# One quarter of a batch's denominators inverted on GpSimd by a power instead of on VectorE by a reciprocal

## The chip, the cores and the metric

The kernel runs on one core of one Trainium2 chip. Its time is device microseconds of one execution. Besides timed runs there is one profiled execution, from which all the durations and starts below come; starts count from the first instruction of that execution.

## The reference

The inputs are q, k and v, each of shape 4 x 6080 x 256 (batch, positions, channels), a number tau = 1, and two weight matrices. For each of the four batches the columns of q and k are normalized over the positions, a 256 x 256 matrix of channel products is formed, a softmax is taken over its rows, and v is multiplied by the result. All rows then go through a two-layer network with a tanh-approximated GELU.

```python
qn = q / (np.linalg.norm(q, axis=1, keepdims=True) + 1e-06)
kn = k / (np.linalg.norm(k, axis=1, keepdims=True) + 1e-06)
s = kn.transpose(0, 2, 1) @ qn / tau
s = s - s.max(-1, keepdims=True)
a = np.exp(s)
a /= a.sum(-1, keepdims=True) + 1e-09
x = (v @ a).reshape(B * S, D)                 # 24320 x 256
h = x @ w_in                                  # 24320 x 2048
g = 0.5 * h * (1.0 + np.tanh(c * (h + 0.044715 * h * h * h)))
out = g @ w_out                               # 24320 x 256
```

## The kernel before

**Stages.** The softmax matrix of a batch is small, so the kernel multiplies its exponentials into w_in once per batch (tiles `aw`, lines 454 to 474, scaled by the reciprocal row sums) and then applies the result to v directly. The main loop runs over 48 blocks of 512 positions (12 per batch, the last of each 448 wide). For a block n, TensorE computes the hidden layer from `aw` and the transposed v block (`h`, line 521; some parts by a scheme with fewer products, `rb` and `qp`, line 597), ScalarE applies the GELU, and TensorE multiplies by w_out (`r` and `p`, line 726). VectorE forms the sums and differences that these schemes need, and turns the output blocks round.

**The next batch is prepared meanwhile.** While the blocks of one batch are worked on, the channel products of the next are accumulated from its q and k (line 248, `row` steps). Around the last two blocks of a batch stands a chain of small steps for the next one: the sums of squares (`ss`, `sv`), their square roots as a power 0.5 on GpSimd (`pow`, line 382, 128 x 4 elements), factors (`kf`, `kr`, `krp`), scaled products (`S0`, `S1`) and then the exponentials.

**The exponentials of later batches.** ScalarE has the table of the GELU loaded, which also gives tanh. For batches 1, 2 and 3 the exponential of a score x is therefore formed as (1 + t) / (1 - t) with t = tanh(x / 2), in `scores_c`:

- step `dn` (line 424, ScalarE): the denominators 1 - t, one tile of 128 x 512 float32.
- steps `rc0` to `rc3` (line 434, VectorE): each inverts a quarter of that tile in place, 128 x 128 elements.
- step `eT` (line 429, VectorE): (1 + t) times the inverted denominators, written as bfloat16.

Behind them come `rsum` (line 444, TensorE: the row sums of eT), `rs` (line 450, VectorE: their reciprocals), and the `aw` products (line 461, TensorE), all of which read eT or what comes of it. Batch 0 uses the exponential itself and has none of these steps.

**What sets the order.** The order is written out by hand: for each of the 48 blocks a string lists the steps, and every step issues its instructions at once, so each engine's queue holds them in the order of that list. An engine works through its queue in order and waits at an instruction until what it needs is there. In the three blocks concerned the relevant part of the list is

```
g0 w0cq rc0 w0y5 ... M1A-1 rc1 y5-1 ... M6A-1 rc2 G3 ... w1m5 rc3 w1m1 ... w1y5 eT w1m6 ... rsum+1 ...
```

(batch 1; `dn` is the third step before the end of the block before. In batches 2 and 3 `dn` and `rc0` to `rc3` stand in the same block as `eT`.)

**GpSimd's queue** holds, apart from the three square roots, the issues of DMAs: q and k tiles of the next batch (line 99, `lq` and `lk`) and the copies of v blocks into bfloat16 (line 153, `lv`, four blocks ahead). SyncE's queue holds the transposing loads of v (line 163) and the output stores (line 816).

Of the kernel before, what the change touches and what calls it, by code (L numbers as in the profile page):

```python
# [11 lines left out]
FP32 = mybir.dt.float32  # L12
BF16 = mybir.dt.bfloat16
AF = mybir.ActivationFunctionType
ALU = mybir.AluOpType
# [3 lines left out]
def kernel(  # L19
# [10 lines left out]
    nc = tc.nc  # L30
# [17 lines left out]
    const = ctx.enter_context(tc.tile_pool(name="const", bufs=1))  # L48
# [369 lines left out]
    def scores_c(b, step):  # L418

        th = TH[b]  # L420
        if step == 0:
            dn = smx.tile([128, 2, 256], FP32, tag="S", name=f"dn{b}")
            DN[b] = dn
            nc.scalar.activation(dn, th, AF.Copy, scale=-1.0, bias=1.0)
            return
        dn = DN[b]
        if step == 5:
            eT = smx.tile([128, 2, 256], BF16, tag="eT")
            nc.vector.scalar_tensor_tensor(eT, th, 1.0, dn, op0=ALU.add, op1=ALU.mult)
            ET[b] = eT  # L430
            return
        step -= 1
        piece = dn[:, step // 2, step % 2 * 128 : step % 2 * 128 + 128]
        nc.vector.reciprocal(piece, piece)

    DN = {}

# [383 lines left out]
    with tc.manual_schedule():  # L821
# [12 lines left out]
        nc.vector.memset(eps, 1e-12)  # L834
        halves = const.tile([128, 4], FP32)
        nc.vector.memset(halves, 0.5)
        log_it = const.tile([128, 1], FP32)
        nc.vector.memset(log_it, math.log(inv_tau))
        ident_bf = const.tile([128, 128], BF16)
# [45 lines left out]
        for f0, f1 in ((0, 256), (256, 512), (512, 1024), (1024, 1536), (1536, 2048)):  # L885
# [14 lines left out]
            "gc": g_copy, "ss": ss_cols, "sv": norms, "pow": roots, "kf": k_factors, "kr": k_row,  # L900
            "krp": k_row_pe, "rsum": row_sums, "rs": row_factors,
            "dn": lambda b: scores_c(b, 0), "eT": lambda b: scores_c(b, 5),
        }
        for i in range(2):
# [4 lines left out]
        for i in range(4):  # L909
            CHAIN[f"rc{i}"] = lambda b, i=i: scores_c(b, i + 1)  # L910
# [327 lines left out]
```

## Time and profile before

| | |
|---|---|
| timed runs | 696.82 and 696.54 us, median 696.68 |
| span of the profiled execution, first to last instruction | 695.2 us (the profile gives no other time for this execution) |
| instructions | 14413 |
| mean granted TensorE clock | 0.998 |
| TensorE busy | 677.3 us, 5501 matmuls |
| VectorE busy | 630.8 us, 1245 instructions |
| ScalarE busy | 616.0 us, 894 instructions |
| GpSimd busy | 73.4 us, 135 instructions |

The two timed runs lie 1.5 us above the span at their median; what lies outside the span is before the first and after the last instruction. In the lines of the profile PE is TensorE, PEld its weight loads, DVE VectorE, ACT ScalarE, POOL GpSimd and SP SyncE; `L434` is line 434 of the kernel; `out<-in` are the names of its tiles. A number in square brackets in a timeline is how long the engine was idle before the instruction and, behind the arrow, what ended that idleness. A line of "..." marks lines left out.

### The profile page before, as it was taken

How to read it: one execution, taken by the hardware profiler on the slowest of the kernel's cores; microseconds unless marked ns; L12 is line 12 of the kernel's file. 1: busy time of each engine (PE TensorE's matmuls, PEld its weight loads, DVE VectorE, ACT ScalarE, POOL GpSimd, SP SyncE). 2: the span in 40 equal slices, each digit the busy share in tenths (PEclk: the TensorE clock that was granted, in tenths of full speed). 3: DMA queues.
4: the chain of work that ended last, by engine and by line, in shares of the span. 5: the costliest groups of instructions: out<-in, count | busy, mean ns of one | idle time of the engine just before them, and what ended most of it. 6: DMA issues, size and time to landing. Idle time of an engine off the chain costs nothing.

```text
span 695.2 us, 14413 instructions
## 1 busy us (share of the span) xinstructions
PE 677.3 (97%) x5501; PEld 530.7 (76%) x5501; DVE 630.8 (91%) x1245; ACT 616.0 (89%) x894; POOL 73.4 (11%) x135
## 2 busy tenths in 40 slices
PE   3999999999999999999999999999999999999996
PEld 2857787777778777777777777777877888888785
DVE  3579998999998889999999889999999999999996
ACT  5389989999889999999988999999888999999993
POOL 4321101111001001101010100010000000000000
PEclk9999999999999999999999999999999999999999
DMA  9996888897478777747587777593563463453325
GB/s 240 207 269 98 160 141 126 114 150 109 65 144 126 130 120 105 122 80 121 91 138 121 119 120 126 97 141 53 83 99 69 77 103 61 81 103 59 54 39 89
DMA packets 161462, 79.07 MB, mean 114 GB/s; under 512 B 148448, under 2 KB 152160, under 8 KB 160672
## 3 DMA queue, kind: packets, MB, share of 16 engines
q0 software_dynamic: 14448, 39.72, 34.2%
q1 hardware_dynamic: 145696, 37.14, 31.8%
q10 hardware_dynamic: 1248, 1.28, 0.6%
q8 instruction: 43, 0.70, 0.4%
q14 instruction: 27, 0.22, 0.1%
HBM read 78.91 MB, written 36.57 MB: 166 GB/s over the span
## 4 chain that ended last, share of the span: by engine, by line
PE 95%; DMA 4%; DVE 0%; issue 0%; POOL 0%; ACT 0%; DVEq 0%; POOLq 0%
PE r L726 24%; PE h L521 22%; PE p L726 18%; PE rb L597 13%; PE qp L597 10%; PE G L248 5%; DMA t<-in_k_dram 2%; PE awp L461 2%; DMA t<-in_q_dram 1%; PE ss L282 0%; PE ss L275 0%; PE vt_ps L325 0%; PE rk L406 0%; PE warm L370 0%; DVE vT_pe L331 0%
## 5 line engine op out<-in xcount | busy, mean ns | idle before, releaser
L726 PEld LDWEIGHTS <-wcomb 128*128 128x128 bf16 x2688 | 261.9, 98 | 43.5 <-issue 0.2
L531 ACT ACTIVATE g<-h 128x1024 bf16<-128x1024 f32 (+1 forms) x178 | 179.9, 1014 | 16.4 <-PE h L521 13.9
L726 PE MATMUL r<-t,wcomb 128*128 128x256 bf16 (+1 forms) x1152 | 163.6, 272 | 0.1
L521 PE MATMUL h<-vT,aw 128*128 128x512 bf16 (+1 forms) x624 | 158.6, 377 | 0.0
L623 ACT ACTIVATE g<-qp 128x1024 bf16<-128x1024 f32 (+1 forms) x103 | 104.7, 1016 | 7.3 <-PE qp L597 5.8
L726 PE MATMUL p<-g,wcomb 128*128 128x256 bf16 (+1 forms) x760 | 108.0, 272 | 0.0
L521 PEld LDWEIGHTS <-aw 128*128 128x128 bf16 x712 | 69.2, 98 | 49.4 <-DVE aw L364 0.6
L597 PEld LDWEIGHTS <-sw 128*128 128x128 bf16 x824 | 80.2, 98 | 25.5 <-issue 1.3
L193 ACT ACTIVATE sq<-t 128x1536 bf16<-128x1536 bf16 (+4 forms) x59 | 79.2, 1359 | 6.2 <-DMA t<-in_q_dram 6.0
L618 DVE TENSOR_TENSOR qp<-rb,yw 128x512 f32<-128x512 f32 (+1 forms) x103 | 70.8, 688 | 12.3 <-PE rb L597 9.5
L597 PE MATMUL rb<-tv,sw 128*128 128x256 bf16 (+1 forms) x412 | 78.0, 271 | 0.2 <-DVE qp L618 0.2
L621 DVE TENSOR_TENSOR xw<-rb,yw 128x512 f32<-128x512 f32 (+1 forms) x103 | 69.5, 674 | 3.9 <-PE rb L597 2.4
L613 ACT ACTIVATE qp<-rb 128x512 f32<-128x512 f32 (+1 forms) x103 | 59.7, 580 | 11.9 <-PE rb L597 6.8
L597 PEld LDWEIGHTS <-aw 128*128 128x128 bf16 x618 | 60.3, 98 | 12.7 <-issue 0.7
L631 ACT ACTIVATE g<-xw 128x512 bf16<-128x512 f32 (+1 forms) x103 | 63.4, 626 | 1.3 <-DVE xw L621 1.2
L616 ACT ACTIVATE yw<-qp 128x512 f32<-128x512 f32 (+1 forms) x103 | 61.2, 594 | 3.7 <-PE qp L597 1.9
L699 DVE TENSOR_TENSOR t<-g,t 128x1024 bf16<-128x1024 bf16 (+1 forms) x96 | 63.4, 668 | 0.6
L701 DVE TENSOR_TENSOR t<-g 128x1024 bf16<-128x1024 bf16 (+1 forms) x96 | 63.8, 673 | 0.0
L703 DVE TENSOR_TENSOR t<-t,g 128x1024 bf16<-128x1024 bf16 (+1 forms) x96 | 63.6, 669 | 0.0
L628 ACT ACTIVATE g<-rb 128x512 bf16<-128x512 f32 (+1 forms) x103 | 61.2, 596 | 2.2 <-PE rb L597 1.7
L248 PE MATMUL G<-t 128*128 128x256 bf16 (+1 forms) x352 | 60.1, 279 | 0.1
L687 DVE TENSOR_TENSOR t<-g 128x2048 bf16<-128x2048 bf16 (+1 forms) x48 | 57.5, 1197 | 0.0
(137 smaller groups left out, 890.0 us busy)
## 6 DMA issues: line engine op xcount, KB each, us to landing
out_dram<-ot SPq DMA_DIRECT2D x174, 128.0 KB, 3.2
vb<-in_v_dram POOLq DMA_DIRECT2D x41, 256.0 KB, 4.2
t<-in_q_dram POOLq DMA_DIRECT2D x21, 384.0 KB, 4.9
t<-in_k_dram POOLq DMA_DIRECT2D x21, 384.0 KB, 5.8
wst<-in_moe_w_out_dram POOLq DMA_DIRECT2D x2, 1024.0 KB, 11.0
t<-in_q_dram POOLq DMA_DIRECT2D x3, 512.0 KB, 14.4
t<-in_k_dram POOLq DMA_DIRECT2D x3, 512.0 KB, 17.2
out_dram<-ot SPq DMA_DIRECT2D x12, 112.0 KB, 2.6
```

The lines of the kernel that those rows point to most:

```text
L193: nc.scalar.activation(o, t[:np_, r, :], AF.Square)
L248: nc.tensor.matmul(G[b][:, jc, :], lhsT=qt[:np_, r, jc * 128 : jc * 128 + 128], rhs=kt[:np_, r, :], start=first and jc == 0, stop=jc == 1, ...
L521: mm = nc.tensor.matmul(hp[:, u, :cols], lhsT=AW[b][:, cc, fc * 128 : fc * 128 + 128], rhs=vt_tiles[n][:, cc, :cols], start=cc == 0, stop= ...
L531: nc.scalar.activation(gs(n)[:, 2 * p : 2 * p + 2, :cols], HP.pop((n, p))[:, :, :cols], AF.Gelu_apprx_tanh)
L597: GATE[0] = nc.tensor.matmul(acc[:, u * hc : u * hc + hc], lhsT=lhs[:, u * 128 : u * 128 + 128], rhs=rhs, start=m in (1, 5) and u == 0, st ...
L618: nc.vector.tensor_add(qp(n, i)[:, 1, :c], RB[n, i][:, :c], YW[n, i][:, :c])
L621: nc.vector.tensor_add(XW[n, i][:, :c], RB[n, i][:, :c], YW.pop((n, i))[:, :c])
L623: nc.scalar.activation(gs(n)[:, 2 * pa : 2 * pa + 2, :c].rearrange("p u (t x) -> p t u x", t=2), QP.pop((n, i))[:, :, :c].rearrange("p t ( ...
L631: nc.scalar.activation(gs(n)[:, 2 * pb : 2 * pb + 2, hc:c], two(XW.pop((n, i))[:, :c]), AF.Gelu_apprx_tanh)
L701: nc.vector.tensor_sub(o, quarter(n, 1, 1, f0, f1), quarter(n, 0, 1, f0, f1))
L703: nc.vector.tensor_sub(o, ts[2][:, f0:f1, :hc], quarter(n, 1, 0, f0, f1))
L726: nc.tensor.matmul(ACCS[n, acc][:, :hc], lhsT=wcomb[:, w, fc, :], rhs=x, start=first and k == 0, stop=k == 3, skip_group_check=True)
```

## The change

In each of batches 1, 2 and 3 the first quarter of the denominators (step `rc0`) is inverted by GpSimd, as a power with exponent -1, and no longer by VectorE's reciprocal. The exponents are a constant tile of 128 x 128 elements, filled with -1 once at the start by VectorE. The other three quarters and all other steps stay; `rc0` stays at its place in the hand-written order. On GpSimd's queue the power thus stands in front of the DMA issues that follow it in that order, and `eT` now needs a result of GpSimd besides those of VectorE and ScalarE.

```diff
@@ scores_c
         step -= 1
         piece = dn[:, step // 2, step % 2 * 128 : step % 2 * 128 + 128]
-        nc.vector.reciprocal(piece, piece)
+        if step == 0:
+            nc.gpsimd.tensor_tensor(piece, piece, minus, op=ALU.pow)
+        else:
+            nc.vector.reciprocal(piece, piece)
@@ constants
         nc.vector.memset(halves, 0.5)
+        minus = const.tile([128, 128], FP32)
+        nc.vector.memset(minus, -1.0)
```

## Prediction

> **What bounds the kernel now.** I read the page's busy shares and chain first: they say which engine sets the end.
>
> ```profile
> PE 677.3 (97%) x5501; PEld 530.7 (76%) x5501; DVE 630.8 (91%) x1245; ACT 616.0 (89%) x894; POOL 73.4 (11%) x135
> ...
> PE 95%; DMA 4%; DVE 0%; issue 0%; POOL 0%; ACT 0%; DVEq 0%; POOLq 0%
> ```
>
> TensorE is busy for 677.3 of 695.2 us and is 95% of the chain that ended last. VectorE works 91% but almost never ends a wait on that chain, and GpSimd is nearly free. So VectorE time taken away is worth little, while a stop that reaches TensorE is paid in full: its queue is in order, and it has only 17.9 us of idle time in the whole span.
>
> Next, the tile view of the denominators (dn), and then that of rt, which the only power on GpSimd writes: after the name come the count and the shortest, median and longest duration in ns.
>
> ```profile
> L434 DVE RECIPROCAL dn<-dn x12: 894/942/954, 176.2 to 514.8; 128x128 f32<-128x128 f32 x12
> L424 ACT ACTIVATE dn<-th x3: 627/630/631, 175.5 to 508.8; 128x512 f32<-128x512 f32 x3
> L429 DVE SCALAR_TENSOR_TENSOR eT<-th,dn x3: 644/669/692, 182.8 to 516.9; 128x512 bf16<-128x512 f32 x3
> ```
>
> ```profile
> L382 POOL TENSOR_TENSOR rt<-sv,halves x3: 1028/1037/1049, 167.3 to 494.4; 128x4 f32<-128x4 f32 x3
> ```
>
> The reader is to see two durations side by side: a reciprocal of 128 columns takes VectorE 0.94 us; a power of four columns takes GpSimd 1.037 us.
>
> Last, the timeline around the first of the three batches (start and duration in us).
>
> ```profile
> 176.18 0.95 DVE L434 RECIPROCAL dn<-dn 128x128 f32<-128x128 f32 x1
> 177.29 0.70 DVE L618 TENSOR_TENSOR qp<-rb,yw 128x512 f32<-128x512 f32 x1 [0.16 <-ACT yw L616]
> ...
> 180.43 0.53 POOL L99 DMA_DIRECT2D t<-in_q_dram  x1 [10.23 <-ACT g L623]
> ...
> 182.57 0.51 POOL L153 DMA_DIRECT2D vb<-in_v_dram  x1 [1.62 <-PE rb L597]
> 182.80 0.64 DVE L429 SCALAR_TENSOR_TENSOR eT<-th,dn 128x512 bf16<-128x512 f32 x1
> ...
> 183.66 0.24 PE L444 MATMUL sums<-ones_bf,eT 128*128 128x1 bf16 x4
> ```
>
> The first piece is inverted at 176.18, as soon as ScalarE's dn is done (175.52 + 0.63 = 176.15), and its consumer eT starts at 182.80. TensorE reads eT for the row sums at 183.66, having waited 0.2 us for it (the tile view's figure). Behind that read the chain has no slack.
>
> **Part by part.**
>
> *Removed:* three reciprocals of 0.94 us on VectorE, 2.8 us in all. In the first batch VectorE then waits 0.16 us for ScalarE's yw anyway, and TensorE is the chain, so of these 2.8 us I count a gain of 0; the ends are 0 and -2.8.
>
> *Added, a constant:* one fill of 128x128 with -1 at the start. The fills of that size beside it take 0.17 us, and VectorE then idles 4.0 us for ident. Nothing; uncovered it would be 0.17.
>
> *Added, three powers of 128x128 on GpSimd.* No row shows one, so its duration d is bounded. From below: all of the 1.037 us is a fixed price, and more columns cost what they cost a plain GpSimd fill: 0.10 us at one column, 0.273 at 128, so 0.0014 us each; d = 1.04 + 124 x 0.0014 = 1.2 us. From above: everything is per column, d = 1.037 x 32 = 33.2 us. The rows nearest to the fixed price are the one-column fill (0.10) and ident's select of 128 columns (0.29 in all). With 0.10 fixed, a column costs 0.234 us and d = 30.0; with 0.29, 0.187 and d = 24.2. I take the middle, **d = 27 us**, because rows of simple work show that starting an instruction on GpSimd costs 0.1 to 0.3 us; the other 0.75 or more must be arithmetic of four columns, unless the power has a long preamble of its own. No row excludes one.
>
> *The new wait.* Square root's power started 0.09 us after its input (sv ended at 167.19), so the first batch's power starts at 176.25. The eT instruction now waits for it, and it stands in VectorE's in-order queue; TensorE's next instruction that needs eT, the row sums, stands in TensorE's. Both engines stop, and with them ScalarE and all that waits for products. Cover is the time from the power's start to eT's old start, less 0.1 for the signal: 182.80 - 176.25 - 0.1 = 6.45 us in the first batch; in the others (dn done at 343.64 and 509.45, eT at 351.20 and 516.87) 7.36 and 7.22. With d = 27 the delays are 20.55, 19.64 and 19.78: 60.0 us. In the second and third batch TensorE came to the sums 0.1 and 0.2 us after eT; less 0.3 gives 59.7.
>
> *TensorE after a stop.* The timeline's start shows what idleness does to it.
>
> ```profile
> 16.88 3.73 PE L248 MATMUL G<-t 128*128 128x256 bf16 x16
> ...
> 22.08 1.91 PE L248 MATMUL G<-t 128*128 128x256 bf16 x16
> ```
>
> The same sixteen matmuls take 3.73 us and later 1.91. Up to 14.98 us it worked in short bursts; working without pause from then on, it kept the slow rate until about 20.2: 5.2 us at half rate lose 2.6. After a stop of 20 us I add that three times: 7.8 (ends 0 and 7.8).
>
> *Queued behind the power on GpSimd* are DMA issues: t from q (180.43 before) and vb (182.57). They leave after 203.3, against 180.43 + 20.55 = 201.0 had they moved with everything else: 2.3 us late. The next squaring of a q tile is at 216.88, and vb is transposed a window (some 14 us) later. Nothing; without that cover, up to 2.3 us a batch. SyncE's queue holds nothing that moves.
>
> *Sharing between VectorE and GpSimd.* [...]
>
> ```profile
> 167.28 1.05 POOL L382 TENSOR_TENSOR rt<-sv,halves 128x4 f32<-128x4 f32 x1 [4.62 <-DVE sv L376]
> ...
> 167.84 0.68 DVE L701 TENSOR_TENSOR t<-g 128x1024 bf16<-128x1024 bf16 x1
> ```
>
> L701 reads two tiles and starts in the middle of the power. It takes 0.68 us, against 0.673 in the mean, and the power 1.05 against 1.03 and 1.04 in the batches where nothing of that kind overlapped it. So I count 0 for contention. [...]
>
> [...]
>
> **Sum.** 0 + 0 + 59.7 + 7.8 + 0 = 67.5 us on the profiled span of 695.2: 762.7. The median of the two timed runs, 696.68, is 1.5 above that span, so **764 us**, slower by 9.7%. With d = 24.2 it is 756, with 30.0 773, with 33.2 783; without the slow restart 756.
>
> **Rivals.**
>
> *A: the power costs mostly a fixed price (not slower).* For: the row has only one size, and a preamble of 0.8 us would explain it; GpSimd is idle 89%. Against: no other GpSimd row shows so dear a start. It decides at d = 6.45 us, or 0.044 us a column: below that the wait is covered, and the time is 696.7 with at most 2.8 gained: 694 to 697, likeliest 696.4, as TensorE's wait of 0.2 us is what could go.
>
> *B: in between, 0.05 to 0.16 us a column.* A loop that overlaps columns would give, say, d = 11: delays 4.55 + 3.64 + 3.78 = 12.0, and with stops this short perhaps no slow restart: 709. At d = 20, 39 + 7.8: 743. It covers 700 to 750.
>
> [...]
>
> *D: TensorE's clock does not fall* is inside the forecast's range: 756.
>
> **Chances.** Forecast 0.55 (d of 24 to 33 without exclusion: 748 to 783, counting restarts of 0 to 2.6 us), A 0.20, B 0.12, C 0.13. Within 2%, about what a measurement of this kernel can tell from no change (682.7 to 710.6), lies A and the lower end of B: 0.22. Slower 0.77. Faster would need 14 us from a VectorE that gives up 2.8: 0.01. The range: 695 to 787. It takes in A, since its 0.20 is too much to leave out beside the upper tails, and all of B and C but C's dearest end; the likeliest case alone is 748 to 783.
>
> **What would show it.** In the profile after: a row of three GpSimd powers of 128x128 near 27 us each; a wait of VectorE's eT on it of some 20 us, three times, and of TensorE's L444 behind it; slices of the span with lower busy digits at 176, and later twice more; half-rate matmuls after each. [...] If the power takes under 6.4 us, the forecast is wrong at its first step.

## The result and the profile after

The changed kernel takes 744.21 us (743.47 and 744.94) against 696.68: a ratio of 1.068, interval 1.065 to 1.071. Timed again in four executions it took 744.58 us, ratio 1.069 (1.067 to 1.070). The profiled execution has a span of 741.6 us where the kernel before had 695.2: 46.4 us more.

The page of the kernel after, its busy shares, the 40 slices of the span for TensorE, VectorE, GpSimd and TensorE's granted clock, and the chain that ended last:

```profile
PE 683.4 (92%) x5501; PEld 533.6 (72%) x5501; DVE 629.0 (85%) x1243; ACT 616.3 (83%) x894; POOL 135.7 (18%) x138
...
PE   3999999998399999999849999999966999999996
...
DVE  4589998997398899999739898999946999999997
...
POOL 4411011106601001101651001010083000000000
PEclk9999999999699999999969999999997999999999
...
PE 86%; POOL 8%; DVE 2%; DMA 1%; ACT 1%; issue 0%; SPq 0%; DVEq 0%; POOLq 0%; ACTq 0%
```

There are three holes in TensorE and VectorE; at each of them GpSimd is busy, and in the slice in which each hole ends TensorE's granted clock (the share of its full clock that it was allowed, `PEclk`) is down to 6 or 7 tenths. GpSimd, which was on none of the chain, has 8% of it: 62.4 us, the three powers. TensorE has the same 5501 matmuls.

The tile view of dn, the instructions that write it and eT (count, and shortest, median and longest in ns):

```profile
L437 DVE RECIPROCAL dn<-dn x9: 912/942/945, 177.6 to 545.8; 128x128 f32<-128x128 f32 x9
...
L435 POOL TENSOR_TENSOR dn<-dn,minus x3: 20802/20802/20803, 175.9 to 540.6; 128x128 f32<-128x128 f32 x3
L429 DVE SCALAR_TENSOR_TENSOR eT<-th,dn x3: 691/691/691, 196.8 to 561.4; 128x512 bf16<-128x512 f32 x3
```

And who waited for whom, in us in total, number of times, and the longest:

```profile
PEld L447 <- DVE eT L429: 41.4, 3, 14.3
DVE eT L429 <- POOL dn L435: 41.1, 3, 14.2
PE sums L447 <- DVE eT L429: 40.3, 3, 14.0
```

A power of 128 x 128 takes 20.80 us, 22 times the reciprocal that it replaces. eT waits 41.1 us for the three of them, and the row sums wait 40.3 us for eT. (Lines behind the edit have moved by three: the row sums are L447 here, L444 before.)

The timeline around the first batch, as before the change:

```profile
175.95 20.80 POOL L435 TENSOR_TENSOR dn<-dn,minus 128x128 f32<-128x128 f32 x1 [6.01 <-ACT dn L424]
...
178.48 0.63 DVE L702 TENSOR_TENSOR t<-g,t 128x1024 bf16<-128x1024 bf16 x1
...
180.48 0.63 DVE L704 TENSOR_TENSOR t<-g 128x1024 bf16<-128x1024 bf16 x1
...
196.73 0.60 POOL L99 DMA_DIRECT2D t<-in_q_dram  x1
196.78 0.69 DVE L429 SCALAR_TENSOR_TENSOR eT<-th,dn 128x512 bf16<-128x512 f32 x1 [14.19 <-POOL dn L435]
...
197.53 0.27 PE L447 MATMUL sums<-ones_bf,eT 128*128 128x1 bf16 x4 [13.99 <-DVE eT L429]
```

VectorE reaches eT early and stands 14.19 us; TensorE stands 13.99. Until then nothing is disturbed: VectorE's instructions that read two tiles in the middle of the power (L702, L704) take 0.63 us, against 0.67 in the mean.

The windows view of the stop and of the 10 us behind it; the number behind the last bracket is the granted clock:

```profile
core 0: us, PE busy (x) PEld busy (x) DVE busy (x) ACT busy (x) POOL busy (x), PEclk, DMA share, GB/s
183.00:196.00 13.00, 0.55 (x5) 0.24 (x3) 0.00 (x0) 1.22 (x2) 13.00 (x1) 0.68 0.00 0
196.00:206.00 10.00, 8.47 (x53) 5.46 (x54) 8.07 (x17) 4.90 (x7) 2.38 (x4) 0.74 0.56 91
```

In the same view of the kernel before it is 1.00 around all three places (176 to 184, 343 to 353 and 509 to 519 us).

### The profile page after: what moved, and what is told of

Same layout as the page of the kernel before. It is cut to its first block, busy times and chain, and to the rows that moved or that the text cites. A ratio compares the mean times of both kernels' runs of the same rounds, so it can differ in the third digit from the quotient of the medians.

```text
span 741.6 us, 14419 instructions
## 1 busy us (share of the span) xinstructions
PE 683.4 (92%) x5501; PEld 533.6 (72%) x5501; DVE 629.0 (85%) x1243; ACT 616.3 (83%) x894; POOL 135.7 (18%) x138
## 4 chain that ended last, share of the span: by engine, by line
PE 86%; POOL 8%; DVE 2%; DMA 1%; ACT 1%; issue 0%; SPq 0%; DVEq 0%; POOLq 0%; ACTq 0%
PE r L729 21%; PE h L524 19%; PE p L729 16%; PE rb L600 12%; PE qp L600 9%; POOL dn L435 8%; PE G L248 6%; PE awp L464 2%; DMA qk_f<-in_q_dram 1%; PE warm L370 1%; PE ss L275 1%; PE ss L282 0%; DVE eT L429 0%; ACT sq L193 0%; PE ss L269 0%
## 5 line engine op out<-in xcount | busy, mean ns | idle before, releaser
L524 PE MATMUL h<-vT,aw 128*128 128x512 bf16 (+1 forms) x624 | 160.6, 381 | 0.0
L621 DVE TENSOR_TENSOR qp<-rb,yw 128x512 f32<-128x512 f32 (+1 forms) x103 | 70.8, 687 | 14.1 <-PE rb L600 10.4
L153 POOL DMA_DIRECT2D vb<-in_v_dram x45 | 22.7, 504 | 278.2 <-PE rb L600 191.7
L435 POOL TENSOR_TENSOR dn<-dn,minus 128x128 f32<-128x128 f32 x3 | 62.4, 20802 | 25.7 <-ACT dn L424 25.7
L702 DVE TENSOR_TENSOR t<-g,t 128x1024 bf16<-128x1024 bf16 (+1 forms) x96 | 63.3, 666 | 0.6
L704 DVE TENSOR_TENSOR t<-g 128x1024 bf16<-128x1024 bf16 (+1 forms) x96 | 63.6, 671 | 0.0
```

The source lines that it names most:

```text
L435: nc.gpsimd.tensor_tensor(piece, piece, minus, op=ALU.pow)
L524: mm = nc.tensor.matmul(hp[:, u, :cols], lhsT=AW[b][:, cc, fc * 128 : fc * 128 + 128], rhs=vt_tiles[n][:, cc, :cols], start=cc == 0, stop= ...
L621: nc.vector.tensor_add(qp(n, i)[:, 1, :c], RB[n, i][:, :c], YW[n, i][:, :c])
L704: nc.vector.tensor_sub(o, quarter(n, 1, 1, f0, f1), quarter(n, 0, 1, f0, f1))
```

## The experiments

The diffs of experiments 1 to 4 are against the changed kernel, that of 5 against the kernel before. The additional constant tiles that some of them need, among them `spare`, which nobody reads, are left out of the diffs.

**1. The power without its reader.** Does the time go to the wait of eT alone, or does a power of 20 us also hurt by being there?

```diff
         if step == 0:
-            nc.gpsimd.tensor_tensor(piece, piece, minus, op=ALU.pow)
-        else:
-            nc.vector.reciprocal(piece, piece)
+            nc.gpsimd.tensor_tensor(spare, th[:, 0, 0:128], minus, op=ALU.pow)
+        nc.vector.reciprocal(piece, piece)
```

> Edit: VectorE inverts all four pieces again; beside them GpSimd still raises 128 x 128 elements (a quarter of tanh's tile, at about the same moment) to the power -1, into a spare tile that nobody reads. Theory W (the loss is the wait of eT for the power, nothing else): the powers still take 20.8 us each, VectorE's two-input instructions beside them keep 0.67 us, and the time is 696 to 698 us. Rival C (a power shuts VectorE out while it reads): VectorE stands for 15 to 20 us per batch whether or not it needs the result, and the time is 725 us or more. A third possibility, the DMA issues that stand behind the power on GpSimd's queue (q tile and v block, 14 to 16 us late without a shift of the rest): if they matter, TensorE or ScalarE waits for a DMA after each power, and the time is 699 to 715 us.

Measured: 696.63 us, ratio 1.000 (0.999 to 1.001). The three powers ran, 20.8 to 21.3 us each, and cost nothing; TensorE's only wait for a DMA that the kernel before does not have, 0.9 us, lies at 28.7 us, long before the first power. The timeline of this run:

```profile
174.28 0.67 DVE L703 TENSOR_TENSOR t<-g 128x1024 bf16<-128x1024 bf16 x1
174.31 21.30 POOL L435 TENSOR_TENSOR spare<-th,minus 128x128 f32<-128x128 f32 x1 [4.47 <-ACT th L416]
...
175.24 0.64 DVE L701 TENSOR_TENSOR t<-g,t 128x1024 bf16<-128x1024 bf16 x1
...
178.39 0.63 DVE L701 TENSOR_TENSOR t<-g,t 128x1024 bf16<-128x1024 bf16 x1
...
180.39 0.63 DVE L703 TENSOR_TENSOR t<-g 128x1024 bf16<-128x1024 bf16 x1
```

So the loss is the wait. Rival C (VectorE shut out) falls, and with it the DMA issues that stand behind the power: here they were late without a shift of the rest (the q tile behind the first power left at 195.60 us, 180.43 before), and nobody noticed.

**2. Fewer columns on GpSimd.** Three kernels give GpSimd the first 32, 48 or 64 columns of the piece and VectorE the others; the edit is that of 32.

```diff
         if step == 0:
-            nc.gpsimd.tensor_tensor(piece, piece, minus, op=ALU.pow)
+            nc.gpsimd.tensor_tensor(piece[:, 0:32], piece[:, 0:32], minus[:, 0:32], op=ALU.pow)
+            nc.vector.reciprocal(piece[:, 32:128], piece[:, 32:128])
         else:
             nc.vector.reciprocal(piece, piece)
```

> Edit: GpSimd inverts only 32 of the piece's 128 columns by the power, VectorE the other 96. With the two sizes seen so far (4 columns 1.03 us, 128 columns 20.80) a column costs 0.159 us and the start 0.40, so 32 columns take 5.5 us, less than the cover of 6.4 to 7.4 us. Theory W: eT waits for nothing, the time is 696.0 to 697.3 us, no different from before. Rival S (the price goes in coarse steps or depends on the values, so that the two sizes don't give a line): over 6.5 us, and eT waits; at 20.8 us 744 us.

> Edit: GpSimd inverts 48 of the piece's 128 columns by the power, VectorE the other 80. By the line (0.39 + 0.159 a column) 48 columns take 8.0 us, 1.6 us more than the cover in the first batch, 0.7 and 0.8 more in the others. Theory W: eT waits 3.0 us in all; if stops of 1 to 2 us leave TensorE at its full rate, 699.4 to 700.2 us. If they don't, 1.5 to 2.3 us a batch more: 704 to 706.

> Edit: GpSimd inverts 64 of the piece's 128 columns by the power, VectorE the other 64. By the line 64 columns take 10.6 us. Theory W: eT waits for 10.6 less the cover, 3.2 to 4.2 us a batch, 10.5 us in all; 707 us if TensorE keeps its rate over stops this short, up to 712 us if it restarts slowly (1.5 us each). Rival S: the wait is not 3 to 4 us. Rival C: more than 712 us.

Measured: 696.73 us with 32 columns (ratio 1.000, 0.999 to 1.001), 699.38 with 48 (1.004, 1.003 to 1.005), 710.62 with 64 (1.020, 1.019 to 1.022). The power's line in the tile views of the three kernels, in this order:

```profile
L435 POOL TENSOR_TENSOR dn<-dn,minus x3: 5452/5455/5455, 175.9 to 509.2; 128x32 f32<-128x32 f32 x3
```

```profile
L435 POOL TENSOR_TENSOR dn<-dn,minus x3: 8048/8049/8050, 175.8 to 511.1; 128x48 f32<-128x48 f32 x3
```

```profile
L435 POOL TENSOR_TENSOR dn<-dn,minus x3: 10574/10574/10575, 175.7 to 517.6; 128x64 f32<-128x64 f32 x3
```

With 5.46 us eT waits for nothing, as the cover of 6.45 to 7.36 us says. With 8.05 it waits 2.8 us in all and the kernel is 2.8 us slower. With 10.57 it waits 10.4 us, but the kernel is 14.0 us slower at its median (the profiled execution, 709.85 us, is 13.3 slower): the price of a slow restart has come in. The timeline of TensorE in the kernel with 64 columns shows one:

```profile
187.03 0.25 PE L448 MATMUL sums<-ones_bf,eT 128*128 128x1 bf16 x4 [3.76 <-DVE eT L429]
187.14 0.60 PE L730 MATMUL r<-t,wcomb 128*128 128x256 bf16 x4
187.63 0.38 PE L601 MATMUL rb<-tv,sw 128*128 128x256 bf16 x2
187.85 1.71 PE L525 MATMUL h<-vT,aw 128*128 128x512 bf16 x4
189.35 1.06 PE L465 MATMUL awp<-win_bf,eT 128*128 128x512 bf16 x2
```

The first work after the stop is still fast (four matmuls in 0.60 us, as in the kernel before); a microsecond later four matmuls of 512 columns take 1.71 us instead of 1.03. The granted clock is 1.00 from 183 to 188 us, 0.66 in the mean from 188 to 193, and 1.00 again from 193. Measured from the row sums to the start of the second aw product, this batch takes 5.70 us where the kernel before took 187.87 - 183.66 = 4.21: 1.5 lost. The third batch, after a stop of 2.96 us, lost 1.7; the second, after 2.92, only 0.06. With 48 columns TensorE's stops add up to 2.1 us, the longest 1.2, and the time shows no restart.

**3. What sets the price of a power.** Nobody waits in these two kernels; they measure operations on GpSimd, a different one in each batch.

```diff
         if step == 0:
-            nc.gpsimd.tensor_tensor(piece, piece, minus, op=ALU.pow)
-        else:
-            nc.vector.reciprocal(piece, piece)
+            x, y, c = {1: (ones_f, minus, 16), 2: (ones_f, half_f, 128), 3: (th[:, 0, :], half_f, 64)}[b]
+            nc.gpsimd.tensor_tensor(spare[:, 0:c], x[:, 0:c], y[:, 0:c], op=ALU.pow)
+        nc.vector.reciprocal(piece, piece)
```

> Edit: as the first of these runs (nobody waits), but the three powers differ: batch 1 raises 16 columns of ones to -1, batch 2 raises 128 columns of ones to 0.5, batch 3 raises 64 columns of tanh's values (both signs) to 0.5. If the price is a start and a price per column, whatever the numbers: 2.9, 20.8 and 10.6 us. If the values matter (a power of one or of a half, negative bases being quicker or slower): they leave this line by more than 5%. Time 696 to 698 us.

> Edit: as in the first run (all four pieces on VectorE, a GpSimd operation beside them whose result nobody reads), but batch 1 multiplies 128 columns on GpSimd, batch 2 multiplies 4, batch 3 raises 1 column to -1. If the 0.40 us at zero columns belongs to the power: the multiplication of 4 columns takes 0.1 to 0.2 us, and the power of one column 0.56. If GpSimd needs it for any operation with two inputs: the multiplication of 4 takes 0.4. For 128 columns of a multiplication 0.3 to 0.7 us, against the power's 20.8. Time 696 to 697 us.

The tile view of the first:

```profile
L436 POOL TENSOR_TENSOR spare<-ones_f,minus x1: 2945/2945/2945, 170.0 to 170.0; 128x16 f32<-128x16 f32 x1
L436 POOL TENSOR_TENSOR spare<-ones_f,half_f x1: 20831/20831/20831, 334.8 to 334.8; 128x128 f32<-128x128 f32 x1
L436 POOL TENSOR_TENSOR spare<-th,half_f x1: 10641/10641/10641, 508.3 to 508.3; 128x64 f32<-128x64 f32 x1
```

The GpSimd timeline of the second, batches 1 and 2 (multiplications) and 3 (a power of one column):

```profile
174.41 0.95 POOL L436 TENSOR_TENSOR spare<-th,minus 128x128 f32<-128x128 f32 x1 [4.48 <-ACT th L416]
...
340.89 0.19 POOL L436 TENSOR_TENSOR spare<-th,minus 128x4 f32<-128x4 f32 x1 [6.21 <-ACT th L416]
```

```profile
508.19 0.70 POOL L436 TENSOR_TENSOR spare<-th,minus 128x1 f32<-128x1 f32 x1 [9.77 <-ACT th L416]
```

From 16 to 128 columns the price rises by (20.80 - 2.95) / 112 = 0.1594 us a column, and the line meets zero columns at 0.39 us. Bases of one, of both signs, exponents of -1 and 0.5: the values change nothing that shows (20.83 us for ones to the 0.5 beside 20.80, and 10.64 for both signs beside 10.57). A multiplication of four columns takes 0.19 us, so about half of the 0.39 is the power's own. The power of one column took 0.70 where the line says 0.55, and the multiplication of 128 columns 0.95 where 0.3 to 0.7 was expected; both started while a two-input instruction of VectorE was running (see the last section). Both kernels took 696.77 us in a single execution.

**4. TensorE kept busy through the stop.** Is what lies beyond the bare waits the slow rate after a stop, or the refilling of queues?

```diff
-        SUMS[b] = ps = pM.tile([128, 2], FP32, tag="a", name=f"sums{b}")
+        full = pM.tile([128, 512], FP32, tag="a", name=f"sums{b}")
+        for i in range(115):
+            nc.tensor.matmul(full[:, 256:512], lhsT=ones_bf, rhs=zeros_bf, start=True, stop=True)
+        SUMS[b] = ps = full[:, 0:2]
```

> Edit: the changed kernel, with 115 spare matmuls of 256 columns (0.109 us each, 12.5 us a batch, on zeros, into columns of the row sums' bank that nobody reads) in TensorE's queue in front of the row sums, so that TensorE works through most of the stop of 13 to 14 us. Theory R (the time beyond the bare waits is TensorE's slow rate after a stop, 1.5 us a batch): no half-rate matmuls behind the row sums, and 739 to 741 us, 4.5 below the changed kernel's 744.2. Rival P (that time is the refilling of queues and buffers after the stop): no difference, 743.5 to 745.

> The changed kernel as it is, timed again in more rounds, to put its distance to the run with TensorE kept busy (737.5 us) on more than two executions: 743.4 to 745.0 us by the two seen.

Measured: 737.54 us (737.43 to 737.60) against 744.58 (743.62 to 744.96): 7.0 us less, more than the 4.5 expected, by work that serves nothing. TensorE's timeline in this kernel:

```profile
183.34 12.72 PE L446 MATMUL sums<-zeros_bf,ones_bf 128*128 128x256 bf16 x115
197.49 0.25 PE L450 MATMUL sums<-ones_bf,eT 128*128 128x1 bf16 x4 [1.44 <-DVE eT L429]
...
198.31 1.03 PE L527 MATMUL h<-vT,aw 128*128 128x512 bf16 x4
199.18 0.59 PE L467 MATMUL awp<-win_bf,eT 128*128 128x512 bf16 x2
```

and the same place in the changed kernel:

```profile
198.90 1.91 PE L524 MATMUL h<-vT,aw 128*128 128x512 bf16 x4
200.60 0.92 PE L464 MATMUL awp<-win_bf,eT 128*128 128x512 bf16 x2
```

eT waits 41.1 us in both. From the row sums to the second aw product the changed kernel takes 1.5, 2.3 and 2.1 us more than the kernel before in the three batches (5.9 in sum, span 741.6); in the execution profiled again 2.1, 2.6 and 2.2 (6.9, span 742.6); with TensorE kept busy 0.1 in sum, and there the granted clock is 1.00 from 183 to 206 us, through the stop and behind it. What is left of the loss, 735.8 - 695.2 = 40.6 us of span, is no more than the bare wait. So the slow restart is the second term, and it also makes up the microsecond by which these two executions differ. My 1.5 us a batch had been read from the first batch alone, the cheapest.

**5. What there was to win.** The kernel before, with reciprocals left out and nothing in their place: one piece, then all four.

```diff
-        nc.vector.reciprocal(piece, piece)
+        if step > 0:
+            nc.vector.reciprocal(piece, piece)
```

> Edit: the kernel before, with the first piece's reciprocal left out in the three batches (the denominators of that quarter stay as they are, so this part of the computation is missing) and nothing put in its place. It is the best that any cheap way to invert the piece elsewhere could give. If VectorE's time there is covered by TensorE's work: 696.3 to 696.7 us. Rival V (VectorE's queue is what TensorE runs behind in these stretches): up to 2.8 us less, 693.9.

> Edit: the kernel before, with all four pieces' reciprocals left out in the three batches (the inversion of the denominators is missing), 11.3 us of VectorE's work. Covered: 695.9 to 696.7 us. Rival V: up to 11.3 us less, 685.4.

Measured: 697.13 us (ratio 1.0007, 0.9998 to 1.0016) and 696.65 (0.9999, 0.9990 to 1.0008). The first lies 0.4 us above what was expected, within its interval of no difference. VectorE is 9.2 us less busy in the second (621.6 for 630.8), and the span is 695.0 for 695.2. So no way of inverting these pieces, however cheap, could have made this kernel faster by more than about 0.1%; no version beat the kernel before.

## Why the prediction was right, and where its sizes were off

Forecast were 764 us and 695 to 787; the direction, the mechanism and the three places hold. The size does not hold as well: the measured 744.2 us lies 4 us below the likeliest case (748 to 783) and is inside the wide range because that was stretched down to take in the rivals A and B. By its steps:

- **What bounds the kernel, and the relief of VectorE counted as 0.** Right: experiment 5 measures it, for all four pieces.
- **The power's duration, d = 27 us: the mis-sized term.** It is 20.80, below the bounds of 24.2 to 30.0 that I had taken as likely, inside those of 1.2 to 33.2. The step that failed is the fixed price. I took it from GpSimd's one-input rows (0.10 and 0.29), but a power has 0.39 before its first column, and so of the 1.037 us at four columns 0.64 was per column, not 0.75 to 0.94. Multiplying four columns to 128 multiplied that error. The term explains 3 x 6.2 = 18.6 of the 21 us by which the forecast of the span was too high.
- **The new wait, d less the cover.** Right. With d = 20.80 the same working gives 14.35 + 13.44 + 13.58 = 41.4 us; eT waited 41.1, TensorE 40.3. The covers of 6.45, 7.36 and 7.22 were confirmed from both sides by 32 and 48 columns.
- **The slow restart, 7.8 us.** It is there, at 5.9 and 6.9 us in the two profiled executions. The 2.6 each were read from the start of the kernel, where the slow rate lasted 5.2 us. That the size came near is in part luck: in that stretch the profile gives a granted clock of 1.00 throughout, while behind the powers it is 0.50, so it is not shown that the two slow rates are the same thing. Case D, a clock that does not fall, is out.
- **The sum, made again** with what was measured: 40.1 (TensorE's 40.3 less the 0.2 of before) + 5.9 = 46.0 of 46.4 us.
- **The DMA issues behind the power, and the fill of the constant: nothing.** Right, experiment 1.
- **Rival A, a price that is mostly fixed:** fell. Its point of decision, 6.45 us, lies at (6.45 - 0.39) / 0.1594 = 38 columns.
- **Rival B, a smaller price per column:** the measured 0.16 is just its upper end, and its case of d = 20 (743 us) came nearest to the time. I had given it 0.12, against 0.55 for 24 us and more.
- **Rival C, VectorE shut out while a power reads:** fell. Six of VectorE's two-input instructions ran inside a power in 0.63 to 0.68 us, against 0.67 in the mean: L702 and L704 of the changed kernel, the three of experiment 1 from 175.24 us on, and L701 in the forecast's row. No run shows the time that the upper end of the range, 787 us, adds for this rival; in experiment 1 the powers ran beside VectorE at a ratio of 1.000.

## What to carry to other kernels

An idle engine is free only as long as nobody needs its result sooner than it comes (here 696.63 us with no reader, 744.21 with one): before moving an operation, take its duration at the new size, and the time from its earliest start to its reader, and put the difference on the path of every in-order queue behind that reader (here 41.1 us on VectorE's, 40.3 on TensorE's). When a duration must be stretched from a small size to a large one, the split between start and slope decides (0.39 us and 0.159 a column for this power); measure one larger size beside the kernel, with no reader, which cost nothing here (696.63 us, ratio 1.000). And before offloading a busy engine, leave the work out once: if the time does not fall (here 696.65 us with all four reciprocals left out, ratio 0.9999), there is nothing to win.

## What the runs showed of the hardware that I had not expected

**Four powers that started beside a two-tile instruction of VectorE took 0.07 to 0.50 us longer; the four VectorE instructions kept their 0.67 to 0.68 us.** In experiment 1 the first power lasted 21.30 us, 0.50 more than the others' 20.80, and began 0.03 us after a two-input instruction of VectorE (174.28); the third lasted 0.13 more and began 0.41 after one (508.08 and 507.67). In the kernel of sizes, 64 columns took 10.64 instead of 10.57, begun 0.48 after one; the power of one column, 0.15 over its line, 0.41 after one. In all four the work seems to have begun 0.53 to 0.56 us after VectorE's instruction did. The second power of experiment 1, which began beside an instruction that reads one tile and a bank of PSUM, lasted 20.80. That it is the reading that is waited for was not tried by itself.

**TensorE's granted clock changed in steps of 3.41 us.** Read in windows of 0.1 us around the three stops of the changed kernel, the granted clock is 1.00 or 0.50. It halves at 187.60, 371.92 and 552.82 us, 3.8 to 4.3 us after TensorE stopped, and is full again 13.65 us later each time, 3.7 to 4.8 us after work resumed. The falls lie 184.32 and 180.91 us apart; the difference, 3.41, goes 54 and 53 times into them and four times into the 13.65. With 64 columns the clock was halved for about as long as one such step, behind two of the stops: 0.66 in the mean of 188 to 193 us is half a clock for 3.4 of 5 us, and by the starts of the matmuls, as an estimate, it fell at about 188.05 and 529.4 us, when TensorE had been working again for about 1.0 and 0.5 us; that is why the first 0.8 us of work behind the first stop were still fast. The second stop there brought no fall (behind it four matmuls of 448 columns took 0.92 us, as at the full clock), although it is only 0.04 us shorter than the third (2.92 and 2.96 us). Counted on from those two falls in steps of 3.41 us, again an estimate, the third lies almost whole inside one step, and the second is cut by the border of two into about 1.7 and 1.3. So the price of a restart, 1.5 to 2.6 us, should depend on where in a step the work resumes; that was not tried by itself.
